# Two H3 and FFN layers on one core: block 1's odd spectra kept as doubled halves, h in two transfers, variances moved to VectorE

## The chip, the cores and the metric

The kernel runs on one core of a Trainium2 chip. The core has five engines that run in parallel, each with its own instruction queue in order: TensorE (matmuls, PE in the profile; its weight loads are shown as PEld), VectorE (DVE), ScalarE (ACT), GpSimd (POOL) and SyncE (SP), which here issues nearly all DMA transfers. Matmuls write to PSUM; VectorE or ScalarE bring the result to SBUF. The metric is the device time of one execution in microseconds; lower is better.

## The reference

A sequence of 2048 rows of 512 channels goes through two identical layers. Each is an H3 block (a gated long convolution) and a gated FFN, each behind a layer norm and added to x.

```python
    def _A_ref(q, k, v, shift_k, ssm_k, ssm_D):
        ...
        for t in range(ks):
            k_shift = k_shift + k_pad[:, t:t + S, :] * shift_k[:, ks - 1 - t][None, None, :]
        kv = k_shift * v
        ...  # y = causal convolution of kv with ssm_k along the sequence, by FFT of length 2 S
        y = y + kv * ssm_D[None, None, :]
        return q * y

    def _B_ref(x, w_gate, w_up, w_down):
        return (_silu(x @ w_gate) * (x @ w_up)) @ w_down

    x = A_q
    x = x + _A_ref(_layernorm(x, axis=-1), A_k, A_v, A_shift_k, A_ssm_k, A_ssm_D)
    x = x + _B_ref(_layernorm(x, axis=-1), B_w_gate, B_w_up, B_w_down)
    x = x + _A_ref(_layernorm(x, axis=-1), A_k, A_v, A_shift_k, A_ssm_k, A_ssm_D)
    x = x + _B_ref(_layernorm(x, axis=-1), B_w_gate, B_w_up, B_w_down)
```

The convolution y depends on k, v and the filters alone, not on x, so the kernel computes it once and uses it in both layers. S is 2048, D is 512, F is 1792, and the taps number 4.

## The kernel before, in words

**Blocks and units.** The sequence is cut into 4 blocks of 512 rows (`c` = 0 to 3; the title's block 1 is the first, index 0 in the code). A block is held as 128 partitions of 4 rows each. An FFN unit `(layer, c, h)` is two of the four rows, 256 positions: `h` = 0 the even rows 0 and 2, `h` = 1 the odd rows 1 and 3. There are 16 units; in program order block c gives (0,c,0), (0,c,1), (1,c,0), then the prologues of block c+1 in layer 0, then (1,c,1).

**The convolution.** It is done block against block with transforms as matmuls: `fwd` and `inv` are cosine and sine tables, built on the chip (L1099 to L1113, and transposed by DMA at L1158). A spectrum has four slots of a real and an imaginary part, each 128 x 512; slots 0 and 2 make one pair, 1 and 3 the other. `half` (L431) transforms two of the four rows of a block at a time: parts a and c for slots 0 and 2, b and d for slots 1 and 3, two matmuls for each part. `butterfly` (L445, L447) makes the two slots of a pair from their halves as sum and difference. `direct` (L458) makes a slot without halves, with four matmuls for each part. `product` (L642, L646, and L653 to L667 for whole spectra) multiplies the spectrum X of kv with the spectrum G of the filter into Z. `inverse_half` (L791, L797) forms in `m` the sums and differences of Z's pairs and transforms them back. The even rows need only the sums, the odd rows only the differences.

**Block 0.** Its filter h arrives by `load_h` (L342) in one transfer of 512 KB, ahead of k, v and x on SP's queue; TensorE turns it (`transpose_h`, L477) and k (`transpose_k`, L366), and multiplies the shifted k by diagonal tap matrices `dg` (`shift_mul`, L510). With `H0 = 'half'` the filter spectrum is made from halves; with `X0 = 'direct'` all four slots of X are made directly. `prologue(0, 0, 0, True)` then makes the input zT of the first unit from the even rows, turning z on TensorE (L920); other units turn z by DMA (L893). Later blocks' convolutions (`conv`) run beside the FFN of the blocks ahead of them.

**Layer norm.** `ln_stats` has VectorE gather statistics (L809, L810), add epsilon (L812), and GpSimd raise to the power -1/2 (L814, result `rstd`). `ln_stats_act`, for eight of the norms, has ScalarE do sums and squares (L828, L834) and finish the variance into `ve` (L838) ahead of GpSimd (L840).

**FFN.** For each pair of F-tiles, eight matmuls for gate and eight for up into PSUM tiles `pf` (L311); ScalarE evacuates (L970, L974), VectorE multiplies (L977), and TensorE projects down (L990). The last unit's last row goes out in two column halves, one finished by VectorE (L1008), one by ScalarE (L1011).

**Order.** Nothing is scheduled on the chip. Every operation is entered by `add`, in program order, with its engine, planned cost and buffers; `ORDER` gives each operation its rank, and each engine's queue is the operations of that engine by rank. `Plan.order` also runs through the ranks with the planned costs (`cost`, and `lat` for a transfer), which decides the buffer slot that a tile gets. `Plan.issue` fills planned TensorE gaps in the first 32 us with warm-up matmuls (`warm`, L1267) on a tile `wz`.

Of the kernel before, what the change touches and what calls it, by code (L numbers as in the profile page):

```python
# [9 lines left out]
P = 128  # L10
F32 = mybir.dt.float32
# [5 lines left out]
LN_EPS = 1e-5  # L17
# [13 lines left out]
LK0 = 4.3  # L31
HQ = 'taps'
X0 = 'direct'
# [9 lines left out]
H_SPLIT = False  # L43
# [7 lines left out]
LASTV = True  # L51
ORDER = [
# [85 lines left out]
class Plan:  # L138
# [78 lines left out]
    def issue(self, seq, place, when, warm_until, warm):  # L217
        t, busy = 0.0, {}
        for o in seq:
            start, end = when[o]  # L220
            if o.eng == "PE":
                if start < warm_until and start - t > 0.5:
                    for ring, i in [(r, i) for r in ("pf", "pd", "pc") for i in range(self.rings[r])]:
                        if busy.get((ring, i), 0.0) <= t:
                            n = int((start - max(t, 0.3) - 0.3) / 0.106)
                            if n > 0:
                                warm(ring, i, n)
                            break
# [10 lines left out]
def kernel(  # L239
# [85 lines left out]
    def fT(f, r):  # L325
        return fwd.t[:, BI[f, r], :]
# [974 lines left out]
```

## Time and profile before

| | |
|---|---|
| times of three runs | 344.28, 346.92, 723.23 us; median 346.92 |
| profiled execution | 344.93 us, of which the span from first to last instruction is 343.2 |
| granted TensorE clock | 1.00 |
| TensorE (PE) | 336.4 us busy, 98% of the span |
| VectorE (DVE) | 283.4 us busy, 83% |
| ScalarE (ACT) | 253.9 us busy, 74% |
| GpSimd (POOL) | 35.3 us busy, 10% |
| gate and up matmuls, L311 | 1792 of 256 columns |
| down matmuls, L990 | 440 seen, 102.4 us busy |

Busy time counts an instruction from its start to its end as the profile models them; neighbours on one engine overlap by a little, so the step from one to the next is shorter than one instruction's duration. In the group lines, `out<-in` are the program's tile names and `x` is a count. A wait line gives engine, line and tile that waited, then what ended it, the total in us, the number of times and the longest. A window line gives for each engine its busy time in that stretch, in the order PE, PEld, DVE, ACT, POOL, then the granted clock, the share of the DMA engines and GB/s. A timeline line gives start, duration, engine, line, operation and count; in brackets the idle time before it and what ended it.

### The profile page before, as it was taken

The numbers are of one execution on the slowest core, as the hardware profiler recorded it, in microseconds if no ns is written. First come the engines' busy times: TensorE is split into PE (matmuls) and PEld (weight loads), VectorE is DVE, ScalarE is ACT, GpSimd is POOL, SyncE is SP. The second block draws the span as 40 slices with busy tenths as digits, with TensorE's granted clock in tenths as the row PEclk, the third lists the DMA queues.
The fourth block names the chain that finished last, engine by engine and source line by source line (L and its number), as shares of the span: only waits on it lengthen the run. The fifth ranks groups of instructions, "written<-read, shape, count | busy, mean of one in ns | idle before, by whom it ended". The sixth has DMA issues, their size and how long they took to land.

```text
span 343.2 us, 6553 instructions
## 1 busy us (share of the span) xinstructions
PE 336.4 (98%) x2579; PEld 248.6 (72%) x2610; DVE 283.4 (83%) x482; ACT 253.9 (74%) x504; POOL 35.3 (10%) x46
## 2 busy tenths in 40 slices
PE   8999999999999999999999999999999999999996
PEld 7756868768687676858586777768685877777783
DVE  8899999899999999899999999989998433726022
ACT  6999999899997765958789995779475464446261
POOL 4010100203111000103110100201101001000000
PEclk9999999999999999999999999999999999999999
DMA  7999218310116044040101014210101100110101
GB/s 273 336 316 341 52 27 112 77 32 0 34 31 94 14 95 138 2 94 3 32 2 46 2 46 79 76 32 1 32 0 33 35 13 0 39 39 8 24 26 37
DMA packets 42088, 22.95 MB, mean 67 GB/s; under 512 B 33861, under 2 KB 39882, under 8 KB 42058
## 3 DMA queue, kind: packets, MB, share of 16 engines
q1 hardware_dynamic: 41904, 22.47, 26.6%
q8 instruction: 20, 0.33, 0.4%
q14 instruction: 10, 0.08, 0.1%
q10 hardware_dynamic: 154, 0.07, 0.1%
HBM read 12.33 MB, written 2.10 MB: 42 GB/s over the span
## 4 chain that ended last, share of the span: by engine, by line
PE 91%; ACT 4%; DVE 3%; issue 1%
PE pf L311 54%; PE pd L990 28%; PE ps L311 6%; PE ps L458 1%; ACT H L419 1%; PE wm L1267 1%; DVE bnst L809 1%; ACT hs L487 1%; PE pt L477 1%; ACT X L419 0%; ACT n L859 0%; PE pt L366 0%; DVE m L540 0%; DVE t L665 0%; DVE Z L667 0%
## 5 line engine op out<-in xcount | busy, mean ns | idle before, releaser
L311 PE MATMUL pf<-zT,wu_sb 128*128 128x256 bf16 x896 | 110.4, 273 | 0.1
L311 PE MATMUL pf<-zT,wg_sb 128*128 128x256 bf16 x896 | 110.2, 273 | 0.2
L990 PE MATMUL pd<-wd_sb,ht 128*128 128x512 bf16 (+1 forms) x440 | 102.4, 372 | 1.2
L311 PEld LDWEIGHTS <-wu_sb 128*128 128x128 bf16 x896 | 87.7, 98 | 16.4
L311 PEld LDWEIGHTS <-wg_sb 128*128 128x128 bf16 x896 | 87.6, 98 | 16.5 <-issue 0.8
L974 ACT CAST ht<-pf 128x512 bf16<-128x512 f32 x112 | 64.0, 591 | 29.3 <-PE pf L311 29.1
L970 ACT ACTIVATE sg<-pf 128x512 bf16<-128x512 f32 x112 | 65.5, 603 | 17.4 <-PE pf L311 15.1
L990 PEld LDWEIGHTS <-ht 128*128 128x128 bf16 x462 | 45.2, 98 | 42.5
L977 DVE TENSOR_TENSOR ht<-ht,sg 128x1024 bf16<-128x1024 bf16 (+1 forms) x64 | 39.0, 617 | 24.0 <-ACT sg L970 18.7
L814 POOL TENSOR_TENSOR rstd<-ve,nhalf 128x2 f32<-128x2 f32 x24 | 23.0, 958 | 217.8 <-DVE ve L812 207.6
L1034 ACT CAST dn<-pd 128x512 bf16<-128x512 f32 x30 | 17.0, 589 | 21.0 <-PE pd L990 20.9
L809 DVE BATCH_NORM_STATS2 bnst<-xc 128x6 f32<-128x512 bf16 x48 | 31.6, 684 | 0.6
L419 ACT ACTIVATE X<-ps 128x512 bf16<-128x512 f32 x32 | 19.2, 611 | 4.0 <-PE ps L311 3.4
L653 DVE TENSOR_TENSOR t<-X,G 128x2048 bf16<-128x2048 bf16 x18 | 21.9, 1218 | 0.1
L657 DVE TENSOR_TENSOR t<-X,G 128x2048 bf16<-128x2048 bf16 x18 | 21.9, 1216 | 0.0
L1037 DVE TENSOR_TENSOR xc<-xc,dn 128x1024 bf16<-128x1024 bf16 x15 | 10.3, 689 | 13.4 <-ACT dn L1034 13.2
L665 DVE TENSOR_TENSOR t<-t,t 128x2048 bf16<-128x2048 bf16 x12 | 14.7, 1222 | 0.3
L667 DVE TENSOR_TENSOR Z<-Z,t 128x2048 bf16<-128x2048 bf16 x12 | 14.6, 1220 | 0.2
L840 POOL TENSOR_TENSOR rstd<-ve,nhalf 128x2 f32<-128x2 f32 x8 | 8.7, 1088 | 59.2 <-ACT ve L838 59.1
L419 ACT ACTIVATE H<-ps 128x512 bf16<-128x512 f32 x24 | 13.8, 610 | 0.1
L886 DVE TENSOR_TENSOR n<-n,Yk 128x1024 bf16<-128x1024 bf16 x15 | 10.3, 688 | 4.1 <-ACT n L859 3.8
L604 ACT ACTIVATE kc<-kTb,tapF 128x512 bf16<-128x512 bf16 x16 | 12.1, 783 | 0.0
(105 smaller groups left out, 323.3 us busy)
## 6 DMA issues: line engine op xcount, KB each, us to landing
hn<-in_A_ssm_k_dram SPq DMA_DIRECT2D x4, 512.0 KB, 4.1
vt<-in_A_v_dram SPq DMA_DIRECT2D x4, 512.0 KB, 5.9
xc<-in_A_q_dram SPq DMA_DIRECT2D x4, 512.0 KB, 5.3
out_dram<-xc SPq DMA_DIRECT2D x15, 128.0 KB, 1.8
wg_sb<-in_B_w_gate_dram SPq DMA_DIRECT2D x1, 1792.0 KB
wu_sb<-in_B_w_up_dram SPq DMA_DIRECT2D x1, 1792.0 KB, 8.5
wd_sb<-in_B_w_down_dram SPq DMA_DIRECT2D x1, 1280.0 KB, 12.0
kn<-in_A_k_dram SPq DMA_DIRECT2D x1, 512.0 KB, 4.5
```

Source lines behind the costliest of these rows:

```text
L311: nc.tensor.matmul(o, lhsT=lhsT, rhs=rhs, start=(n == 0), stop=(n == len(terms) - 1))
L419: add("ACT", act(D), lambda: nc.scalar.activation(out=view(), in_=ps.t[:], func=ACT.Copy, scale=scale), r=[ps], w=[(buf, keys)], conv=conv)
L653: dve(n * D, lambda t1=t1, part=part: nc.vector.tensor_mul(out=t1.t[:], in0=x.t[:, sl, 0, :], in1=g.t[:, sl, part, :]), [(x, key(slots, (0 ...
L657: dve(n * D, lambda t2=t2, part=part: nc.vector.tensor_mul(out=t2.t[:], in0=x.t[:, sl, 1, :], in1=g.t[:, sl, 1 - part, :]), [(x, key(slots ...
L665: dve(n * D, lambda t1=t1, t2=t2, comb=comb: nc.vector.tensor_tensor(out=t1.t[:], in0=t1.t[:], in1=t2.t[:], op=comb), [t2], [t1], conv=conv)
L809: add("DVE", 0.6, lambda st=st, i=i: nc.vector.bn_stats(out=st.t[:], in_=xs[c].t[:, i, :]), r=[(xs[c], (i,))], w=[st])
L814: add("POOL", pw, lambda: nc.gpsimd.tensor_tensor(out=rstd.t[:], in0=ve.t[:], in1=nhalf.t[:].to_broadcast((P, n)), op=ALU.pow), r=[ve, nha ...
L970: add("ACT", act(D), lambda ps=ps, o=o, sg=sg: nc.scalar.activation(out=sg.t[:, o:o + 2, :], in_=ps.t[:], func=ACT.Silu), r=[ps], w=[(sg, ...
L974: add("ACT", act(D), lambda ps=ps, o=o, ht=ht: nc.scalar.copy(out=ht.t[:, o:o + 2, :], in_=ps.t[:]), r=[ps], w=[(ht, (o // 2,))], due=(uni ...
L977: dve(n * W, lambda sg=sg, ht=ht: nc.vector.tensor_mul(out=ht.t[:], in0=ht.t[:], in1=sg.t[:]), [sg], [ht], due=(unit, k / pairs, 0.0, "h"))
L990: nc.tensor.matmul((pds[o] if not cs.start else pds[HP]).t[:, cs], lhsT=ht.t[:, q, o * P:(o + 1) * P], rhs=wt["d"].t[:, ft, cs], start=(ft ...
L1034: add("ACT", act(D), lambda o=o: nc.scalar.copy(out=dn.t[:, o, :], in_=pds[o].t[:]), r=[pds[o]], w=[(dn, (o,))], due=(unit, 1.0, 3.0, "h"))
```

## The change

- `X0 = 'sum1'`: X of block 0 has slots 0 and 2 made directly as before. For slots 1 and 3 only the halves b and d are made, into `evx`, evacuated with a factor of 2. The halves of the filter, `ev`, are not combined at this point either. `pair_product` multiplies the halves themselves, b with b and d with d, into Z's slots 1 and 3. Their sum is the sum of the true products (the doubling makes up the factor), which is all that the even rows need: `inverse_sums`.
- The odd rows need the difference. `inverse_differences`, entered behind the first prologue, does the two butterflies, forms the product of slot 1 (with X still doubled, so twice the true one), takes the stored sum from it, which leaves the difference, and transforms back; then the two doubled slots of X are halved for later blocks.
- `H_SPLIT = True`: h of block 0 comes in two transfers, the second entered behind the first, and each turn of a row is two groups of transposes.
- `VE_D = True`: the variance of `ln_stats_act` is finished by VectorE.
- `TAIL = 320`: the last row's columns are cut at 320, not 256.
- The warm-up matmuls read a constant of ones in place of the tile `wz`, whose memset goes, and their number is worked out a little differently.
- Planned latencies of h, k, v and x change, and `ORDER` is a new list of 1576 ranks (1568 before).

```diff
-LK0 = 4.3
+LK0 = 3.8
-X0 = 'direct'
+X0 = 'sum1'
-H_SPLIT = False
+H_SPLIT = True
+TAIL = 320
+VE_D = True
 ORDER = [
...
-                            n = int((start - max(t, 0.3) - 0.3) / 0.106)
+                            n = int((start - t - (0.0 if 0.0 < t < 8.0 else 0.3)) / 0.106)
...
+            o = None
             for n in range(2):
...
-                        lat=LH0 - 0.75 if n == 0 else LH0 - 0.45, due=due, after=after)
+                        lat=(2.95, 3.1)[n], due=due, after=[o] if n else after)
...
+    def turn_part(m, pss, rows, slot, first):
+        for r in rows:
+            for part in (0, 1):
+                f, q = next((f, q) for f, q, t, pt in INV_TERMS[r] if t == slot and pt == part)
+                add("PE", pe(1), lambda f=f, q=q, r=r, part=part: nc.tensor.matmul(
+                    pss[r].t[:], lhsT=iT(f, q), rhs=m.t[:, slot, part],
+                    start=first and part == 0, stop=not first and part == 1),
+                    r=[(m, (2 * slot + part,)), inv], w=[pss[r]])
+
+    def inverse_sums(k):
+        y, z = new_y(k), Z[k]
+        m = spectrum("m")
+        pss = {r: new("pd", "ps", [P, D], F32) for r in (0, 2)}
+        for s in (0, 1):
+            dve(2 * D, lambda s=s: nc.vector.tensor_tensor(
+                out=m.t[:, s], in0=z.t[:, s], in1=z.t[:, s + 2], op=ALU.add), [(z, key((s, s + 2)))], [(m, key((s,)))])
+            turn_part(m, pss, (0, 2), s, s == 0)
+        fresh[k] = pss
+        evacuate_y(k, (2,))
+        return m, pss
+
+    def inverse_differences(k, m, pss):
+        z = Z[k]
+        butterfly(ev, G[0], 1, False)
+        butterfly(evx, X[0], 1, False)
+        pss.update({r: new("pf", "ps", [P, D], F32) for r in (1, 3)})
+        dve(2 * D, lambda: nc.vector.tensor_tensor(
+            out=m.t[:, 2], in0=z.t[:, 0], in1=z.t[:, 2], op=ALU.subtract), [(z, key((0, 2)))], [(m, key((2,)))])
+        turn_part(m, pss, (1, 3), 2, True)
+        pair_product(X[0], G[0], z, 1, 1)
+        dve(2 * D, lambda: nc.vector.tensor_tensor(
+            out=m.t[:, 3], in0=z.t[:, 1], in1=m.t[:, 1], op=ALU.subtract), [(z, key((1,))), (m, key((1,)))], [(m, key((3,)))])
+        turn_part(m, pss, (1, 3), 3, False)
+        evacuate_y(k, (1, 3))
+        for slot in (1, 3):
+            dve(2 * D, lambda slot=slot: nc.vector.tensor_scalar(out=X[0].t[:, slot], in0=X[0].t[:, slot], scalar1=0.5, scalar2=None, op0=ALU.mult),
+                [(X[0], key((slot,)))], [(X[0], key((slot,)))])
...
-        add("ACT", TINY, lambda: nc.scalar.activation(out=ve.t[:], in_=sm.t[:, n:2 * n], func=ACT.Identity, scale=1.0 / D, bias=eps.t[:]),
-            r=[(sm, range(n, 2 * n)), eps], w=[ve])
+        if VE_D:
+            add("DVE", 0.08, lambda: nc.vector.tensor_scalar(out=ve.t[:], in0=sm.t[:, n:2 * n], scalar1=1.0 / D, scalar2=LN_EPS,
+                                                             op0=ALU.mult, op1=ALU.add), r=[(sm, range(n, 2 * n))], w=[ve])
...
-    wz = whole("wz", [P, P])
-    add("DVE", 0.07, lambda: nc.vector.memset(wz.t[:], 0.5), w=[wz], due=-80)
+    ones = nc.const_aps.tensor(1.0, (P, P), BF16)
...
+        elif X0 == "sum1":
+            evx = spectrum("evx")
+            direct(vt[0], X[0], "pf", eng(XVE[2:4]), (2,))
+            half(vt[0], evx, "bd", 2.0, "pf", eng(XVE[4:]), False)
...
-        for slots in PAIRS:
+        for slots in PAIRS if X0 != "sum1" else ((0,), (2,)):
             product(0, 0, slots, False)
+        if X0 == "sum1":
+            for slot in (1, 3):
+                pair_product(evx, ev, Z[0], slot, slot)
...
-        if I0 == "half":
+        if X0 == "sum1":
+            m0, pss0 = inverse_sums(0)
+        elif I0 == "half":
             inverse_half(0, (0, 1))
...
     first, stats = prologue(0, 0, 0, True)
+    if X0 == "sum1" and not SUMS:
+        inverse_differences(0, m0, pss0)
...
-            for half_, (eng, cs) in enumerate((("DVE", slice(0, D // 2)), ("ACT", slice(D // 2, D)))):
+            for half_, (eng, cs) in enumerate((("DVE", slice(0, TAIL)), ("ACT", slice(TAIL, D)))):
```

More of the change, by code (lines that the diff above doesn't have):

```diff
@@ L381, in load_v @@
             return add("ACT", 0.45, lambda: nc.scalar.dma_start(out=vt[b].t[:], in_=v_t[:, b]), w=[vt[b]], lat=5.5, due=-69.5, after=[h0])
[L382 removed]
+        return add("SP", 0.6, lambda: nc.sync.dma_start(out=vt[b].t[:], in_=v_t[:, b]), w=[vt[b]], lat=(5.7, 8.6)[b] if b < 2 else 5.5, due=due, after=after)
     def load_x(c, due=None, after=()):
         xs[c] = new("x", "xc", [P, R, D], parts=R + 2)
[L386 removed]
+        return add("SP", 0.7, lambda: nc.sync.dma_start(out=xs[c].t[:], in_=q_t[:, c]), w=[xs[c]], lat=(6.2, 13.0, 5.0, 5.0)[c], due=due, after=after)
     def load_weights(which, due, after=()):
@@ L944, in ffn @@
                 i = row(h, o)
-                halves = (slice(0, D // 2), slice(D // 2, D)) if unit == LAST_UNIT and o == HP - 1 else (slice(0, D),)
+                halves = (slice(0, TAIL), slice(TAIL, D)) if unit == LAST_UNIT and o == HP - 1 else (slice(0, D),)
                 halves = [cs for cs in halves if own(o, cs)]
@@ L982, in ffn @@
                 split = unit == LAST_UNIT and o == HP - 1
-                halves = (slice(0, D // 2), slice(D // 2, D))
+                halves = (slice(0, TAIL), slice(TAIL, D))
                 cols = [[cs] for cs in halves] if last else [halves] if split else [[slice(0, D)]]
@@ L991, in go @@
                                                  start=(ft == 0 and not own(o, cs)), stop=(ft == NF - 1))
-                    add("PE", pe(n) if not last else pe(n, D // 2), go, r=[ht, (wt["d"], (0 if fts[0] == 0 else 1,))],
+                    add("PE", pe(n) if not last else pe(n, css[0].stop - css[0].start), go, r=[ht, (wt["d"], (0 if fts[0] == 0 else 1,))],
                         w=[pds[o]] if not split else [pds[o], pds[HP]] if not last else [pds[HP if css[0].start else o]],
@@ L1189 @@
             butterfly(evx, X[0], 0, False)
+        elif X0 in ("mix", "mix2"):
+            X[0] = spectrum("X0")
+            evx = spectrum("evx") if X0 == "mix" else new("t4", "evx", [P, 4, D], parts=4)
+            direct(vt[0], X[0], "pf", eng(XVE[:2]), (0,))
         else:
@@ L1194 @@
             half(hs, ev, "bd", 2.0 / N, "pf", eng(EVE[4:]), False)
-            butterfly(ev, G[0], 1, False)
+            if X0 != "sum1":
+                butterfly(ev, G[0], 1, False)
         if X0 == "half":
@@ L1266, in warm @@
         for _ in range(n):
-            nc.tensor.matmul(t[:], lhsT=wz.t[:], rhs=wz.t[:], start=True, stop=True)
+            nc.tensor.matmul(t[:], lhsT=ones, rhs=ones, start=True, stop=True)
     with tc.manual_schedule(engines={mybir.EngineType.DVE, mybir.EngineType.Activation, mybir.EngineType.PE,
```

15 lines of the change are left out of this document (10 added, 5 removed), and 116 rows, old and new, of the table ORDER.

## The prediction

> **What bounds the kernel now.** I read the page first (busy time, the 40 slices, the chain of waits), then sums by stage, then VectorE's waits, then the timeline at the first and at the last place where TensorE starts on a new block.
>
> ```profile
> PE 336.4 (98%) x2579; PEld 248.6 (72%) x2610; DVE 283.4 (83%) x482; ACT 253.9 (74%) x504; POOL 35.3 (10%) x46
> ...
> DVE  8899999899999999899999999989998433726022
> ...
> PE 91%; ACT 4%; DVE 3%; issue 1%
> ```
>
> TensorE is busy all the time and makes up 91% of the chain. But VectorE's row of tenths is 8s and 9s up to the 31st slice and falls only then. The sums by stage say it in microseconds:
>
> ```profile
> 34.00:262.00 228.00, 226.85 (x1698) 167.91 (x1718) 220.38 (x338) 186.43 (x374) 25.17 (x24) 1.00 0.21 44
> 262.00:343.20 81.20, 77.64 (x591) 58.21 (x595) 32.16 (x71) 37.91 (x69) 4.76 (x6) 1.00 0.10 27
> ```
>
> The third busy figure is VectorE: 220.38 of 228 us up to 262, then 32.16 of 81.2. So two engines are full up to 262 us, and VectorE has slack only behind that. Its queue is in order, so what is added to it early arrives at 262, unless a wait takes it up. These are its waits up to there:
>
> ```profile
> DVE ht L977 <- ACT ht L974: 1.2, 3, 0.8
> DVE kTb L374 <- PE pt L366: 1.2, 2, 0.6
> DVE z L864 <- POOL rstd L814: 0.9, 1, 0.9
> DVE n L864 <- POOL rstd L814: 0.9, 1, 0.9
> ...
> DVE n L886 <- ACT n L859: 0.6, 1, 0.6
> DVE G L447 <- ACT ev L419: 0.4, 1, 0.4
> DVE ka L608 <- ACT ka L604: 0.4, 1, 0.4
> DVE ht L977 <- ACT sg L970: 0.3, 1, 0.3
> DVE nmr L848 <- POOL rstd L814: 0.3, 1, 0.3
> ```
>
> And this is the place where 262 us counts, the first unit of block 3 in layer 0:
>
> ```profile
> 261.36 0.73 DVE L864 TENSOR_SCALAR z<-xc,mv,rstd 128x512 bf16<-128x512 bf16 x2 [0.87 <-POOL rstd L814]
> ...
> 261.84 2.50 SPq L893 DMA_TRANSPOSE zT<-z  x2
> ...
> 263.98 2.75 PE L990 MATMUL pd<-wd_sb,ht 128*128 128x512 bf16 x12
> ...
> 266.57 1.69 PE L311 MATMUL pf<-zT,wu_sb 128*128 128x256 bf16 x14
> ```
>
> VectorE writes z, SP issues the two transposes, the second at about 263.1 (half of 2.50 behind 261.84); the page gives 2.4 us to landing, so zT is there at 265.5 and TensorE takes it at 266.57. **The slack is 1.0 us.** Behind it stand four units of FFN, a unit being 112 matmuls of 0.109 us and 28 of 0.216 us, 18.2 us: 73 us that nothing shortens. Any lateness of this z over 1.0 us is a later end.
>
> **The change, part by part.** The sum is made against the profiled execution, 344.93 us: 343.2 of span and 1.7 around it. The three times shown are 344.28, 346.92 (the median) and 723.23, so the profiled one stands 0.6% under the median.
>
> TensorE, removed work. Slots 1 and 3 of the spectrum of block 0 took 2 x 2 x 4 = 16 matmuls at L458 and take 4 x 2 = 8 as halves. A step is 0.216 us (20 of them in 4.48 us): -1.73 us. The inverse keeps its 16 matmuls, but the last four of the odd rows (0.86 us) now stand behind the first FFN matmuls in ORDER.
>
> ```profile
> 4.49 1.86 PE L477 MATMUL pt<-ident,hn 128*128 128x128 bf16 x16
> ...
> 14.62 4.48 PE L458 MATMUL ps<-vt,fwd 128*128 128x512 bf16 x20
> ...
> 24.06 1.09 DVE L646 TENSOR_TENSOR Z<-t,t 128x512 bf16<-128x512 bf16 x3
> 25.18 1.89 DVE L791 TENSOR_TENSOR m<-Z 128x1024 bf16<-128x1024 bf16 x3
> ```
>
> VectorE, added work. Steps come from runs of equal instructions: three sums of 1024 end 1.89 us after the first began, one lasts 0.69, so a step is (1.89 - 0.69) / 2 = 0.60; of 512, (1.09 - 0.42) / 2 = 0.34. The product of slot 1 in `inverse_differences` is new: 2 x 0.60 + 2 x 0.34 = 1.88. The butterfly of X is new: 2 x 0.60 = 1.20. That of G is only moved behind. Two halvings of X slots, tensor_scalar of 1024 elements: not in the trace in this shape. Two z of 512 elements take 0.73, so their step is 0.33, and a sum of 1024 takes 0.60; I take 0.46, the middle, as both rows are equally near: 0.92, bounds 0.66 and 1.20. Eight variances now done here: L812, the same form, lasts 0.17 and steps at about 0.08: 0.64, at most 1.36. The memset of wz goes: -0.17. Sum **+4.5 us, bounds 4.2 to 5.5.** The Trainium skill, "VectorE: DVE Perf Modes", section "The perf-mode tier table", lists a tensor_scalar on bf16 in SBUF at about twice the rate of a tensor_tensor (693 against 1224 ns for 2048). By it a halving is an estimated 0.35 us and the sum 4.25; the 1218 ns of L653 here agree for the two-source side.
>
> From the lists of ORDER, read against the operations in program order, VectorE's queue ahead of z of unit (0,3,0) also gains one addition of L1037 (0.6 net). So z meets **5.0 us more VectorE work (4.7 to 6.0)**.
>
> What pays it back. (1) At the head: h in halves lets the first transposes start on 256 KB. The first of the 16 began at 4.49 and they took 1.86, so starting half of them earlier is worth up to 0.9. It costs one more SP issue of 0.45 us, behind which k, v, x, h1, v1, wg and the inverse tables are queued; the DMA engines are full there (share 1.0 from 2.5 us on), so their landing is set by bytes. VectorE's three waits there are 0.6 + 0.6 + 0.4 = 1.6. Against it stands a new wait: the first variance waits in VectorE's queue for ScalarE's second Square and its read, with the products of pair 3 behind it, and these need the new halves that ScalarE evacuates right after. I price it at 0.5 (0 to 1.6) and credit the head with 1.2 (0 to 1.6, and 0 if both h halves land together). (2) Waits on ScalarE from 34 to 262, 1.2 + 0.6 + 0.4 + 0.3 = 2.5 and some of under 0.3 each: a queue that comes later finds these done. I take 2.2 (0 to 2.8). (3) Waits on POOL's rstd, 0.9 + 0.9 + 0.3 = 2.1: these are answers to VectorE's own variance and vanish only where ORDER puts other work in between. It does so at the two long ones (an ht product and the L1037 addition ahead of this z). I take 1.4 (0 to 2.1). Together 4.8 (0 to 6.5), so z is later by 5.0 - 4.8 = **+0.2 us (-1.8 to +6.0)**, and with 1.0 of slack the unit may start 0.8 earlier.
>
> TensorE's own count agrees. In the head VectorE's queue up to z of unit (0,0,0) is 0.6 us shorter (the difference sums and half a butterfly go behind it), and with 1.2 less waiting z comes 1.8 earlier than 31.45; I take the first FFN matmul 1.5 earlier than 33.58. The 0.86 us moved behind it come off again: -0.6. Both ways the end moves by 0.6 to 0.8.
>
> The small parts. The tail: ScalarE's last copy shrinks from 256 to 192 columns (0.37 us now, 0.61 for 512 in rows like it): -0.06, and VectorE's larger piece becomes the peer: -0.05. ScalarE loses 8 x 0.29 = 2.3 us of variances; it is 73% busy or more, and what hides that is TensorE's own queue, so nothing. Warm-up matmuls on a constant start with the barrier instead of behind the memset, 0.2 earlier: nothing, since they end when data comes. Changed lat figures act only through ORDER and slots.
>
> Sum: 344.93 - 0.8 - 0.05 = 344.1; I say **344.0 us**.
>
> **The rivals.**
> Repaid in full (342.0): every wait vanishes and the head gains 3 us. TensorE then saves its 1.73 and 1.2 of head. For it: TensorE waited for VectorE almost nowhere before. Against: the 1.0 us of slack, and VectorE's queue would have to take up 6 us of waits.
>
> Not repaid (349.0): one mechanism at one place, the z of unit (0,3,0). If VectorE still waits as now, z is 5.0 late, TensorE stands 4.0 and the end is 344.93 + 4.0; 349.9 with the upper prices. It is slower from a net lateness of 1.0 us on. For it: two engines full up to 262, and four VectorE chains per block whose gaps of 0.03 us remain. Against: waits on others shrink when one's own queue is late.
>
> The clock (343.1). Warm-up and transposes before 7 us step at about 0.10 us (16 in 1.86, one lasting 0.3), 64 later ones at 0.06 (3.74 us). If earlier warm-up opened the fast step before the h transposes, 24 transposes save 24 x 0.045 = 1.1 us and VectorE's two waits at L374 go: 0.9 under my sum. The Trainium skill, "TensorE: Matmul & The Clock Gate", section "What's actually happening", says the gate opens after a busy window of about 3.4 us that runs free of the program; here the slow step lasted from 1.04 to about 7.2, nearly two such windows, so a start 0.2 earlier may or may not win one.
>
> The split does nothing (345.2): both halves land with the last byte, since k is queued on the same full DMA engines. The head's 1.2 falls away: 344.1 + 1.2 - 0.1.
>
> **How the numbers follow.** My forecast 0.48 (its own range 343.0 to 346.5), repaid in full 0.17, the clock 0.10, no effect of the split 0.05, not repaid 0.20. The range 341.5 to 349.5 leaves out the lower end of the second case and the upper half of the last. About 2% (6.9 us) is what a measurement of this kernel can tell from no change. Faster by more needs under 338: 0.05, out of the full repayment. Slower by more needs 352, z late by 8 us: over my upper price for one unit, but the same squeeze may cost at several; 0.10, out of "not repaid". The same: 0.85.
>
> **What would show it.** In the changed profile: 16 matmuls at the direct line instead of 32, and 8 of halves; VectorE's busy sum at about 288; its waits up to 262 at half of now; first FFN matmul at 32.1; z of unit (0,3,0) at about 261.6 and TensorE's start on it near 265.8; no TensorE gap over 0.5 us before it. A gap of several microseconds there, or at the start of another unit, proves me wrong on the slow side. An end under 342 would mean that VectorE was not the second bound.

## The result, and the profile after

Over 22 runs each the changed kernel took 346.90 us in the median (344.71 to 348.96) and the kernel before 344.44 us (343.59 to 346.92, and one run of 723.23); the ratio is **1.0066, 95% interval 1.0051 to 1.0081**: slower by 2.3 us where 0.9 faster was forecast. The profiled execution took 347.71 us, 345.8 of them span, against 344.93 and 343.2. The median lies inside the outer range of the prediction, 341.5 to 349.5, but no case of which that range was made names what made it late.

The page of the changed kernel, to set beside that of before (engine, busy us, share of the span, instructions; the tenths of the granted clock in 40 slices; the shares of the chain):

```profile
PE 336.7 (97%) x2583; PEld 248.4 (72%) x2615; DVE 285.4 (83%) x497; ACT 251.2 (73%) x496; POOL 38.7 (11%) x46
...
PEclk9899999999999999999999999999999999999999
...
PE 74%; ACT 11%; DVE 10%; DMA 2%; issue 1%; POOL 1%; SPq 0%
```

VectorE has 285.4 us, 2.0 more than before; the forecast said 288. The chain has changed more than the sums: TensorE's share falls from 91% to 74%, a transfer is in it with 2%, and the second slice of the clock row is no longer 9. The sums by stage (PE, PEld, DVE, ACT, POOL, then clock, DMA share, GB/s) say where:

```profile
0.00:34.00 34.00, 29.93 (x285) 21.40 (x290) 28.08 (x71) 26.87 (x56) 5.34 (x15) 0.95 0.98 315
34.00:262.00 228.00, 226.39 (x1696) 167.47 (x1716) 221.97 (x349) 184.26 (x371) 27.90 (x23) 1.00 0.20 44
262.00:345.80 83.80, 80.33 (x608) 59.58 (x612) 35.39 (x79) 40.06 (x72) 5.49 (x8) 1.00 0.11 26
```

Up to 34 us TensorE is busy for 29.93 us (31.95 before) and the clock stands at 0.95. From 34 to 262 the line is that of before: TensorE 226.39 (226.85), VectorE 221.97 (220.38). So in this execution the loss is at the head. TensorE's first 12 us, on the timeline (start, duration, engine, line, operation, count; in brackets the idle time before it and what ended it):

```profile
3.74 1.91 PE L481 MATMUL pt<-ident,hn 128*128 128x128 bf16 x16
5.45 0.66 PE L1335 MATMUL wm<-const-bfloat16-1.0 128*128 128x128 bf16 x6
8.15 1.07 PE L370 MATMUL pt<-ident,kn 128*128 128x128 bf16 x16 [2.04 <-DMA kn<-in_A_k_dram]
...
9.78 2.77 PE L313 MATMUL ps<-hs,fwd 128*128 128x512 bf16 x6 [0.22 <-issue]
```

h's transposes began at 3.74 in place of 4.49, as intended. Then come 6 warm-up matmuls, **2.04 us of nothing until k lands**, 16 fast transposes of k, and six matmuls of 512 columns in 2.77 us, 0.45 us each in place of 0.22. The window lines of these stretches give the clock beside it:

```profile
8.00:10.00 2.00, 1.63 (x18) 1.31 (x20) 1.29 (x2) 1.19 (x3) 0.00 (x0) 0.79 1.03 396
10.00:13.00 3.00, 3.00 (x12) 1.29 (x11) 1.38 (x2) 1.08 (x3) 0.00 (x0) 0.57 1.04 415
13.00:16.00 3.00, 2.95 (x47) 2.68 (x47) 2.40 (x4) 2.76 (x8) 0.00 (x0) 1.00 1.22 391
```

0.79, then 0.57 for three microseconds, then 1.00. The first FFN matmul starts at 35.38 (before: 33.58; forecast: 32.1), and z of unit (0,3,0), at 261.36 before:

```profile
264.17 0.41 DVE L913 TENSOR_SCALAR z<-xc,mv,rstd 128x512 bf16<-128x512 bf16 x1
```

It is 2.8 late, TensorE starts on it at 269.28 in place of 266.57, and the end is 2.6 later. Of that, 1.80 was there at the first FFN matmul, and 2.67 at the second unit (55.81 against 53.14): the difference is that of the inverse matmuls (0.86 us) that were moved behind the first.

### The profile page after: what moved, and what is told of

It reads as the page before. It is cut to its first block, busy times and chain, and to the rows that moved or that the text cites. A ratio compares the mean times of both kernels' runs of the same rounds, so it can differ in the third digit from the quotient of the medians.

```text
span 345.8 us, 6581 instructions
## 1 busy us (share of the span) xinstructions
PE 336.7 (97%) x2583; PEld 248.4 (72%) x2615; DVE 285.4 (83%) x497; ACT 251.2 (73%) x496; POOL 38.7 (11%) x46
## 4 chain that ended last, share of the span: by engine, by line
PE 74%; ACT 11%; DVE 10%; DMA 2%; issue 1%; POOL 1%; SPq 0%
PE pf L313 43%; PE pd L1039 24%; PE ps L313 5%; DMA kn<-in_A_k_dram 2%; DVE bnst L854 2%; ACT ht L1023 2%; ACT sg L1019 1%; ACT n L908 1%; DVE m L544 1%; PE ps L462 1%; DVE t L657 1%; ACT H L423 1%; DVE t L661 1%; ACT X L423 1%; DVE t L669 1%
## 5 line engine op out<-in xcount | busy, mean ns | idle before, releaser
L313 PE MATMUL pf<-zT,wg_sb 128*128 128x256 bf16 x896 | 111.1, 273 | 0.1
L313 PE MATMUL pf<-zT,wu_sb 128*128 128x256 bf16 x896 | 109.2, 273 | 0.5 <-DVE zT L972 0.4
L1039 PE MATMUL pd<-wd_sb,ht 128*128 128x512 bf16 (+2 forms) x440 | 101.8, 372 | 1.1
L313 PEld LDWEIGHTS <-wg_sb 128*128 128x128 bf16 x896 | 87.6, 98 | 17.4 <-issue 0.4
L313 PEld LDWEIGHTS <-wu_sb 128*128 128x128 bf16 x896 | 87.5, 98 | 16.1 <-issue 1.1
L1019 ACT ACTIVATE sg<-pf 128x512 bf16<-128x512 f32 x112 | 66.6, 607 | 31.7 <-PE pf L313 29.9
L1023 ACT CAST ht<-pf 128x512 bf16<-128x512 f32 x112 | 65.3, 591 | 15.4 <-PE pf L313 12.6
L859 POOL TENSOR_TENSOR rstd<-ve,nhalf 128x2 f32<-128x2 f32 x24 | 24.3, 1015 | 213.1 <-DVE ve L857 171.6
L423 ACT ACTIVATE X<-ps 128x512 bf16<-128x512 f32 x28 | 17.2, 626 | 5.7 <-PE ps L313 4.9
L889 POOL TENSOR_TENSOR rstd<-ve,nhalf 128x2 f32<-128x2 f32 x8 | 10.8, 1347 | 62.5 <-DVE ve L884 62.5
L313 PE MATMUL ps<-hs,fwd 128*128 128x512 bf16 x36 | 13.0, 425 | 1.0 <-ACT hs L491 0.7
```

What stands on the lines that cost most here:

```text
L313: nc.tensor.matmul(o, lhsT=lhsT, rhs=rhs, start=(n == 0), stop=(n == len(terms) - 1))
L423: add("ACT", act(D), lambda: nc.scalar.activation(out=view(), in_=ps.t[:], func=ACT.Copy, scale=scale), r=[ps], w=[(buf, keys)], conv=conv)
L859: add("POOL", pw, lambda: nc.gpsimd.tensor_tensor(out=rstd.t[:], in0=ve.t[:], in1=nhalf.t[:].to_broadcast((P, n)), op=ALU.pow), r=[ve, nha ...
L1019: add("ACT", act(D), lambda ps=ps, o=o, sg=sg: nc.scalar.activation(out=sg.t[:, o:o + 2, :], in_=ps.t[:], func=ACT.Silu), r=[ps], w=[(sg, ...
L1023: add("ACT", act(D), lambda ps=ps, o=o, ht=ht: nc.scalar.copy(out=ht.t[:, o:o + 2, :], in_=ps.t[:]), r=[ps], w=[(ht, (o // 2,))], due=(uni ...
L1039: nc.tensor.matmul((pds[o] if not cs.start else pds[HP]).t[:, cs], lhsT=ht.t[:, q, o * P:(o + 1) * P], rhs=wt["d"].t[:, ft, cs], start=(ft ...
```

## The experiments

Theory 1: the second transfer of h makes k late, TensorE waits and then runs slowly. Theory 2: VectorE's added work costs it, unit by unit. Theory 3, added behind the first four runs: GpSimd's rstd is held up behind VectorE. Each kernel stood in one job with the kernel before; the ratio is to that. "k" is k's place among SyncE's transfers and its time from issue to landing in the profiled execution; "clock" counts the runs with a granted share of 0.995 or less over the whole run; "rstd" is the length of that of unit (1,0,0), near 60 us. Single runs of one kernel differ by up to 4.4 us, so the medians decide, and a profiled execution shows one of them. In e6, e10 and e12 the second of SyncE's transfers is a row of 1 KB. The lines of these kernels lie up to 3 beside those of the changed kernel (L311 is its L313).

| run | median us (runs) | ratio, 95% | k: place, us | first FFN | rstd | clock |
|---|---|---|---|---|---|---|
| before, profiled | | | 2nd, 4.5 | 33.58 | 1.79 | |
| after | 346.90 (22) | 1.0066, 1.0051 to 1.0081 | 3rd, 6.4 | 35.38 | 2.20 | 10 |
| e1 one h | 345.87 (12) | 1.0020, 1.000 to 1.004 | 2nd, 4.5 | 31.89 | 2.20 | 0 |
| e2 ev first | 346.65 (12) | 1.0032, 1.0008 to 1.0056 | 3rd, 5.2 | 32.31 | 2.20 | 0 |
| e3 before, split | 346.56 (12) | 1.0052, 1.0029 to 1.0075 | 3rd, 5.7 | 34.37 | 1.80 | 3 |
| e4 more warm-up | 347.21 (12) | 1.0062, 1.0035 to 1.0088 | 3rd, 6.1 | 33.42 | 3.93 | 0 |
| e5 spectra only | 347.76 (6) | 1.0081, 1.0063 to 1.0099 | 2nd, 4.6 | 31.63 | 2.13 | 5 |
| e6 late k | 344.88 (12) | 1.0013, 0.9988 to 1.0039 | 3rd, 4.0 | 31.35 | 2.20 | 3 |
| e7 h on ScalarE | 346.55 (12) | 1.0049, 1.0031 to 1.0067 | 2nd, 4.5 | 33.94 | 2.20 | 2 |
| e8 before, variances | 349.13 (6) | 1.0134, 1.011 to 1.0159 | 2nd, 4.9 | 35.13 | 1.06 | 0 |
| e9 e4 and copy | 346.26 (9) | 1.0051, 1.0034 to 1.0067 | 3rd, 5.7 | 33.07 | 0.69 | 0 |
| e10 e6, ev first | 345.27 (12) | 1.0023, 1.0003 to 1.0043 | 3rd, 6.5 | 32.76 | 3.93 | 0 |
| e11 k between | 346.68 (6) | 1.0066, 1.0043 to 1.009 | 2nd, 4.7 | 34.35 | 3.93 | 0 |
| e12 e10 and copy | 344.67 (11) | 1.0008, 0.9994 to 1.0022 | 3rd, 5.8 | 32.26 | 0.69 | 0 |
| **e13 e1 and copy** | 344.35 (12) | 0.9989, 0.9975 to 1.0003 | 2nd, 4.6 | 31.47 | 0.69 | 0 |
| e14 e13, ev first | 345.03 (12) | 1.0007, 0.9993 to 1.002 | 2nd, 4.8 | 32.31 | 0.69 | 0 |
| e15 after and copy | 347.57 (6) | 1.0074, 1.0046 to 1.0102 | 3rd, 5.8 | 35.57 | 0.69 | 3 |
| e16 e5 and two copies | 344.49 (12) | 1.0005, 0.9993 to 1.0016 | 2nd, 4.6 | 31.64 | 0.69 | 0 |
| **e17 e13 again** | 344.16 (12) | 0.9978, 0.9961 to 0.9994 | 2nd, 4.4 | 32.00 | 0.69 | 0 |
| e18 before and copy | 344.63 (12) | 0.9993, 0.9977 to 1.0009 | 2nd, 4.9 | 33.09 | 0.69 | 0 |

**The first four: which part.** In e1 and e3 one constant is turned and the ranks of h's load and transposes in ORDER follow it.

```diff
e1 (changed kernel)      e3 (kernel before)
-H_SPLIT = True          -H_SPLIT = False
+H_SPLIT = False         +H_SPLIT = True
```

> The changed kernel with one part undone: block 0's h comes in one transfer again (one issue on SyncE ahead of k's, four whole transposes in place of eight halves); all other parts stay. Theory 1 (the head: the second transfer delays k, TensorE waits 2.0 us for it and then runs slowly): k is issued at 1.24 us instead of 1.73 and lands by 6.5 instead of 8.15, the wait of 2.0 us on kn is below 0.7, the first FFN matmul starts at 33.6 or before (35.4 in the changed kernel), and the time is 344.3 to 345.0, at least 1.8 below the changed kernel. Theory 2 (VectorE's added work, met at every unit): the first FFN matmul comes no more than 0.5 earlier and the time is 346.4 to 347.2.

> The kernel before with one part of the change: h in two transfers, the second ahead of k, the four transposes as eight halves; spectra, variances, warm-up operand and tail as before. Theory 1: the loss is in this part alone: k lands 0.5 to 2 us later than in the kernel before, TensorE waits for it, the first FFN matmul starts 1 to 2 us later than 33.58 and the time is 345.4 to 346.4. Theory 2: no VectorE work is added, so the time is 344.0 to 344.8.

The split alone costs the kernel before 0.52%, 1.8 us, as theory 1 had it (346.56 is 0.2 over its range); taking it out of the changed kernel brings the ratio from 1.0066 to 1.0020, 1.6 us. The head of e1 is better than expected and about what the prediction had said:

```profile
6.35 1.06 PE L368 MATMUL pt<-ident,kn 128*128 128x128 bf16 x16
7.25 1.89 PE L311 MATMUL ps<-hs,fwd 128*128 128x512 bf16 x7
```

k's transposes follow h's with no gap, the matmuls of 512 columns behind them run at the full step, and the first FFN matmul comes at 31.89. But e1's median is 345.87, above the 345.0 expected at most: something else costs 1 us.

e2 changes ranks of ORDER alone: the four `half` operations of h's even pair (L435) and their evacuations stand ahead of `transpose_k`.

> The changed kernel, h still in two transfers and k still issued behind both, but in TensorE's order the eight half matmuls of h's even pair (L435, ev) and their evacuations stand ahead of the sixteen transposes of k. Theory 1: k still lands near 8.1, but some 1.8 us of matmuls now lie in the wait: the wait of 2.0 us on kn falls below 0.8, the first FFN matmul starts near 33.9, the time is about 345.3. Theory 2: the first FFN matmul within 0.5 of 35.4 or the gain is given back by unit (0,3,0); the time stays at 346.4 to 347.2.

The wait on k is gone though k took 5.2 us, no run lost the clock, and the first FFN matmul came at 32.31. The ratio fell by a third of a per cent only (1.0066 to 1.0032; the median is 346.65 where 345.3 was expected), while the profiled execution, at 344.62, is one of the best two; what its other runs lack its trace cannot show. e4 keeps TensorE busy without work:

```diff
-LK0 = 3.8
+LK0 = 6.4
```

> The changed kernel with 31 warm-up matmuls instead of 6 between the transposes of h and those of k (k's planned latency 6.4 instead of 3.8), so that TensorE does not stand still while k is under way. Nothing of the work is earlier. If the clock that drops after the idle 2.0 us is a part of the loss, the 512-column matmuls of 9.8 to 12.6 us have a step of 0.22 instead of 0.43, the first FFN matmul comes 1.0 to 1.5 earlier (34.0 to 34.4) and the time is 345.4 to 345.9. If the wait alone is the loss, the first FFN matmul stays at 35.2 to 35.6 and the time at 346.5 to 347.2.

The clock held in all 12 runs and the first FFN matmul came 2.0 earlier, more than expected. Yet the median is 347.21, and the runs fall into two groups, 345.6 to 346.6 and 347.8 to 349.6. In the profiled one, of the upper group, TensorE stood still for 1.27 us at 66.56. The chain there goes back over ScalarE to GpSimd. GpSimd's instruction, then VectorE's at the same time:

```profile
60.19 3.93 POOL L889 TENSOR_TENSOR rstd<-ve,nhalf 128x2 f32<-128x2 f32 x1 [13.86 <-DVE ve L884]
```

```profile
59.95 0.16 DVE L884 TENSOR_SCALAR ve<-sm 128x2 f32<-128x2 f32 x1
60.02 0.68 DVE L561 TENSOR_TENSOR X<-m 128x1024 bf16<-128x1024 bf16 x1
60.62 1.22 DVE L666 TENSOR_TENSOR Z<-t,t 128x2048 bf16<-128x2048 bf16 x1
61.75 0.68 DVE L1026 TENSOR_TENSOR ht<-ht,sg 128x1024 bf16<-128x1024 bf16 x1
62.35 1.22 DVE L661 TENSOR_TENSOR t<-X,G 128x2048 bf16<-128x2048 bf16 x1
```

A reciprocal root of two columns takes 0.69 us where nothing is beside it. Here it took 3.93, and ended 0.6 behind the fourth of VectorE's two-input operations, when VectorE itself had run out of work. In e1 the same instruction took 2.20 and slipped in behind the second of them. The Trainium skill, "SBUF — State Buffer", section "Who interferes with whom", says that a VectorE instruction with two SBUF inputs contends with a GpSimd instruction that reads SBUF, and calls the pair of ports that the two engines share an exclusive lock. The trace agrees: in e4, in e1 and in the kernel before, this rstd ends 0.55 us behind the end of a two-input operation, whichever it got in behind. That several such instructions in a row can keep GpSimd out, and that this changes from run to run, is what these runs add.

**The next four: single parts and the order of transfers.**

```diff
e5, on e1
-VE_D = True
+VE_D = False
e8, on the kernel before
-        add("ACT", TINY, lambda: nc.scalar.activation(out=ve.t[:], in_=sm.t[:, n:2 * n], func=ACT.Identity, ...
+        add("DVE", 0.08, lambda: nc.vector.tensor_scalar(out=ve.t[:], in0=sm.t[:, n:2 * n], scalar1=1.0 / D, ...
```

> The changed kernel with two parts undone: h in one transfer, as in e1, and the eight variances of ScalarE's statistics finished on ScalarE again, each right behind its sums (eps is then needed, as before). What is left of the change are the spectra, the warm-up operand and the tail. Theory 3 (the variance on VectorE is followed at once by VectorE's own two-input operations, and GpSimd's rstd, which reads it, stands still while these run: 3.93 us for the one at 60.2 us in e4, 2.20 in e1, 1.79 in the kernel before): the rstd of 58 to 62 us takes at most 1.8, and the time is 0.5 to 1.0 below e1's 345.87, thus 344.8 to 345.4. Theory 2 (VectorE's added spectra work is what is left of the loss): removing 0.6 us of small VectorE operations changes little, 345.6 to 346.0. If the variances were a gain, as the prediction had it (1.4 us of rstd waits repaid), the time rises to 346.3 or more.

> The kernel before with one part of the change alone: the eight variances of ScalarE's statistics on VectorE, at the same ranks of the order. Theory 3: the eight rstd of line 840 take longer (median 1.00 us and longest 1.79 in the kernel before; 1.31 and 2.20 to 3.93 in kernels with the variances on VectorE), and the time is 0.3 to 1.2 above the kernel before of the same job. The prediction's reading: rstd comes earlier, and the time is 0 to 1.4 below. Theory 2: no difference, since the spectra are not touched.

Neither is a clean answer on the variances, and theory 3 missed both. In e5 the rstd near 60 us still took 2.13 (1.8 at most was expected) and the time lies over every range given but that of the variances as a gain; rstd of unit (0,0,1) took 4.04 us, TensorE stood still for 2.16 at 42.04 and the clock fell to 0.81 from 44 to 50. In e8 the ranks are those of ScalarE's operations, and VectorE waits there for the sums:

```profile
DVE ve L838 <- ACT jk L834: 4.9, 3, 1.8
```

So e8's 4.2 us say more of the place than of the variance; its own rstd near 60 took 1.06 only. In its profiled execution, at 351.0 the slowest of six, the rstd at 112.1 us took 10.53, behind a row of twelve two-input operations of VectorE's.

e6 and e7 ask what delays k.

```diff
e6, on e1
-        dr = add("ACT", 0.42, lambda: nc.scalar.dma_start(out=drow.t[0:1, :], ...
+        dr = add("SP", 0.42, lambda: nc.sync.dma_start(out=drow.t[0:1, :], ...
e7, on the changed kernel
-                o = add(eng, 0.5, lambda sl=sl: q.dma_start(...
+                o = add(("SP", "ACT")[n], 0.5, lambda sl=sl, n=n: (nc.sync, nc.scalar)[n].dma_start(...
```

> e1 (h in one transfer) with one move: the 1 KB transfer of D's row is issued by SyncE between h and k in place of by ScalarE, so that k is issued some 0.5 us later, as in the changed kernel, while h stays whole. If the late issue alone makes k slow, k takes 5.2 to 6.4 us from its issue, as in the four kernels with two transfers, TensorE waits for it and the time is 346.5 to 347.2. If it is the two transfers of h themselves, k takes 4.5 us as in e1, lands 0.5 later than there, TensorE waits at most 0.3 and the time is 345.8 to 346.3.

> The changed kernel with the second half of h issued by ScalarE (behind tapR, ahead of D's row) in place of SyncE, so that k is issued by SyncE at 1.24 us again; h is still two transfers. If the late issue is what delays k, k lands by 6.5, TensorE does not wait for it, and the time is that of e1 or up to 0.5 below, 345.4 to 345.9. If the two transfers themselves slow the DMA engines, k takes over 5.2 us from its issue, lands at 6.5 to 7.5, TensorE waits 0.4 to 1.4 and the time is 346.3 to 347.

e6 by itself spoke for the halves as the cause (k 4.0 us although issued at 1.67), and its median is 0.9 below what was expected for that. But e10 and e12 have the same first transfers as e6, h whole and k third, and k took 6.5 and 5.8 there. In e7 k was in time, 4.5 us; now the half on ScalarE's queue came late, and TensorE waited 0.47 and 1.13 us for h; the time lies in the range for slow halves, but k was not slow. So neither reading held alone, and e11 puts k between the halves: one rank of SyncE's, and the `after` of the second half and of k.

> The changed kernel with SyncE's order h first half, k, h second half. In the four kernels where k was SyncE's third transfer the rate fell to 36 to 121 KB in the half microsecond from 4.0 us, where k's packets begin, against 185 to 206 with h whole. If it is the third large transfer that starts badly, k now takes at most 4.5 us from 1.24 and the second half of h is late (over 4.5 us from its issue at 1.74), TensorE waits for h instead, over 1 us, and the time is 346.3 to 347.3. If the halves themselves are slow, k takes over 5 us again and the time is 347 or more. If neither, both land by 6.2 and the time is 345.0 to 345.9.

k took 4.7 (4.5 expected), the second half, third now, was late, and TensorE waited 1.36 for it; the time is in the range given for "it is the third". Over all profiles: **k as SyncE's second transfer took 4.4 to 4.9 us in eleven of eleven; as its third 5.2 to 6.5 in eight of nine,** and 4.0 in e6. The rate in 40 slices of 0.3 us from 0 to 12 shows the hole, first the changed kernel (with the busy tenths of the DMA engines), then e1:

```profile
DMA  0000002699999923966689999899999999999999
GB/s 0 0 0 0 0 10 72 225 358 359 358 318 174 123 82 150 259 218 205 259 328 382 355 382 369 328 423 393 399 382 396 372 389 420 413 427 403 408 456 401
```

```profile
GB/s 0 0 0 0 0 14 55 133 304 352 341 335 478 410 423 437 341 68 137 246 300 369 423 423 369 396 369 372 386 375 382 430 434 403 399 422 422 415 454 418
```

The 13th to 15th value, from 3.6 us: 174, 123, 82 against 478, 410, 423. In the first two of these slices the engines are busy 9 tenths of the time all the same. There the packets of k, 4096 bytes, begin in the changed kernel; single ones take up to 1213 ns in place of 159. e1 has such a hole too, at the 18th value (68), where v begins, SyncE's third there; nothing waits for v. Why the third transfer starts so is open. A late issue alone is 0.5 us; but in all nine the third place goes together with an issue at 1.67 to 1.74 us in place of 1.24, and no run separates the two.

**GpSimd set free.** One instruction is added: a copy that makes VectorE wait for that rstd.

```diff
+        if key_ == (1, 0, 0):
+            fence = whole("fence", [P, n], F32)
+            add("DVE", 0.1, lambda: nc.vector.tensor_copy(out=fence.t[:], in_=rstd.t[:]), r=[rstd], w=[fence])
         return nm, rstd
```

> e4 (the changed kernel with 31 warm-up matmuls ahead of k) with one added instruction: behind the variance of unit (1,0,0) VectorE makes a 2-column copy of rstd, and so does nothing of its own until GpSimd has finished that rstd. Theory 3 in its general form (GpSimd's rstd stands still while VectorE runs two-input operations back to back; whether it slips in between two of them changes from run to run): the rstd that took 3.93 us from 60.2 takes at most 1.1, the runs of 347.8 to 349.6 of e4 (6 of 12) vanish, and the median falls from 347.2 to 345.7 to 346.4. If the long rstd is not what makes those runs slow, both groups of times stay, 1 us later for the pause of VectorE, and the median is 347 to 348.2.

```profile
59.80 0.69 POOL L887 TENSOR_TENSOR rstd<-ve,nhalf 128x2 f32<-128x2 f32 x1 [13.85 <-DVE ve L882]
...
60.52 0.17 DVE L891 COPY fence<-rstd 128x2 f32<-128x2 f32 x1 [0.80 <-POOL rstd L887]
```

rstd takes 0.69, VectorE pauses for 0.80, and all of e9's runs lie between 346.0 and 346.8: e4's upper group is gone. e10 and e12 repeat it on another base.

> e6 (the changed kernel with h in one transfer and D's row issued by SyncE) with the order of e2: the half matmuls of h's even pair and their evacuations ahead of the transposes of k. Theory 1 with the clock: e6 showed a granted share of 0.995 in 3 of 12 runs, all of them over 347 us, so TensorE still stands still on k in some runs; with work in that place none is left at 0.995, the runs over 346.5 go, and the median falls from 344.9 to 344.0 to 344.6. If these runs have another cause, 2 or 3 of 12 stay over 347 and the median is within 0.4 of 344.9.

> e10 with the one added copy of e9. If the long rstd of unit (1,0,0) comes up in e10 as well, its slow runs go and the median is 0.2 to 0.6 below e10's. If it does not, VectorE's pause of about 1 us costs 0 to 0.8 and the median is at or above e10's.

In e10 five of 12 runs stand at 346.2 to 346.8; the profiled one (346.67) has an rstd of 3.93. In e12 it is 0.69, and the runs span 344.5 to 345.3. So e10's expectation missed: no run was at 0.995, the clock held, and the upper runs were rstd's. The other profiles fit: the third with 3.93, e11's at 348.73, is the only one of its six runs above 346.9, while with 2.20 the profiled executions of e1, e2 and e6 are the fastest or next to it of their kernels.

**Both causes out.** e13 is e1 with the copy, e14 has the order of e2 as well, e15 is the changed kernel with the copy, e16 is e5 with two (`key_ in ((1, 0, 0), (0, 0, 1))`).

> e1 (the changed kernel with h in one transfer, k SyncE's second transfer) with the one added copy of e9 behind the variance of unit (1,0,0). Theory 3: the slow group of e1 (its runs of 346.3 to 347.3) goes; with k early (4.5 us from 1.24) the median is 344.2 to 344.8, at most as in e12, against 345.9 for e1. If k's arrival is all there is, the copy costs up to 1 us and the median is 345.9 to 346.9.

> e13 with the order of e2 (the half matmuls of h's even pair ahead of the transposes of k). With k here by 5.8 us there is no wait left to cover: within 0.3 of e13, with fewer runs above the median if k is late in some runs; 344.2 to 344.8.

> The changed kernel itself with the one added copy behind the variance of unit (1,0,0). Theories 1 and 3 together: the long rstd is gone, but k is still SyncE's third transfer, TensorE still waits for it and the granted share still falls to 0.995 or less in about half of the runs; the median is 345.9 to 346.5, between e9's 346.3 and the changed kernel's 346.9. If theory 3 carries most of the changed kernel's loss, the median is 345.5 or less; if none, 346.9 to 347.9.

> e5 (h in one transfer, the eight variances on ScalarE) with the added copy behind the variances of units (0,0,1) and (1,0,0). e5 lost 2 us against e1, and in its trace the rstd at 35.6 us took 4.04. If that rstd is its whole loss, the variances themselves are worth nothing, and the median is within 0.5 of e13. If the variances on VectorE are a gain of their own, as the prediction had it, the median is 1.0 or more above e13.

e13 is as expected, 344.35. e14 is 0.7 above it, where at most 0.3 was expected: with k in time, the order of e2 only makes k's transposes later (8.0 in place of 5.9). e16 is within 0.5 of e13, so e5's loss was its rstd, with the clock that fell behind it, and **the variances on VectorE are worth 0.1 us by the medians, 0.6 by the ratios**, with one pause of VectorE more in e16. e15 missed: 347.57 with the copy. Three of its six runs lost the clock. In the profiled one the row of the clock shows 9s throughout, but the steps tell more; e15, then e9, which differs by 25 warm-up matmuls:

```profile
5.03 1.26 PE L479 MATMUL pt<-ident,hn 128*128 128x128 bf16 x10 [0.22 <-DMA hn<-in_A_ssm_k_dram]
6.08 0.84 PE L1336 MATMUL wm<-const-bfloat16-1.0 128*128 128x128 bf16 x6
7.62 1.89 PE L368 MATMUL pt<-ident,kn 128*128 128x128 bf16 x16 [0.70 <-DMA kn<-in_A_k_dram]
...
10.16 2.66 PE L311 MATMUL ps<-hs,fwd 128*128 128x512 bf16 x6 [0.22 <-issue]
12.65 0.39 PE L311 MATMUL ps<-dg,kTb 128*128 128x128 bf16 x4
```

```profile
4.52 0.75 PE L479 MATMUL pt<-ident,hn 128*128 128x128 bf16 x10 [0.28 <-DMA hn<-in_A_ssm_k_dram]
5.11 1.99 PE L1336 MATMUL wm<-const-bfloat16-1.0 128*128 128x128 bf16 x31
...
8.43 1.89 PE L311 MATMUL ps<-hs,fwd 128*128 128x512 bf16 x8
```

In e15 ten transposes of h take 1.26, 16 of k 1.89, six matmuls of 512 columns 2.66: the slow step lasts until 12.65. In e9 ten transposes of h take 0.75, 31 warm-up matmuls 1.99 and eight matmuls of 512 columns 1.89: the fast step is there from 4.5 on. That is 2.5 us at the first FFN matmul and 0.8 us by the ratios (1.0074 against 1.0051). So in the changed kernel the wait and the slow step come first, and taking out the long rstd alone gains nothing that six runs show.

> e13 once more, to narrow its interval: if its advantage over the kernel before is real, the median is again 0.1 to 0.6 below that of the kernel before in the same job; if it was chance, within 0.1 or above.

> A control: the kernel before with the added copy of rstd of unit (1,0,0) in VectorE's queue, behind the first product that runs beside that rstd. In the kernel before this rstd took 1.79 us in the profiled execution, and 6 of 35, 1 of 29 and 2 of 29 of its runs stood at 346.5 or more. If the copy helps any kernel of this kind, it also takes these runs away and the median is 0 to 0.4 lower; if the long rstd concerns the changed order alone, the pause of VectorE costs 0 to 1 us and the median is 344.5 to 345.5.

e13 again is faster than the kernel before, 0.9978 with an interval below 1; the two jobs give 0.25 and 0.7 us. The copy alone brings the kernel before nothing that the interval shows.

## Why the prediction was wrong, point by point

**The step that failed is point (1) of the repayment: the second issue of h costs nothing because "the DMA engines are full there, so their landing is set by bytes".** In the profiled execution k landed 2.4 us later (8.1 against 5.7) behind the same bytes. From 3 to 6 us, before the change and after, the last two figures are the share of the DMA engines and GB/s:

```profile
3.00:6.00 3.00, 2.94 (x30) 2.58 (x28) 2.79 (x12) 2.00 (x5) 1.81 (x3) 1.00 1.02 352
```

```profile
3.00:6.00 3.00, 3.00 (x32) 2.63 (x29) 2.85 (x15) 2.66 (x8) 1.80 (x3) 1.00 0.80 215
```

So the engines were neither full nor, where they were busy, moving bytes at their rate: a share of busy time does not say that bytes alone set a landing. The trace of before held the warning: its rate also dips, to 259 GB/s at 5.4 us, where v was SyncE's third transfer. The prediction credited the head with 1.2 and bounded it at 0 from below; the split alone measured 1.8 us of loss. Nor did it read the new ORDER for what stands in TensorE's queue behind a late k: all 16 transposes stood ahead of the matmuls on h, where the kernel before had eight, with matmuls on h in between.

**The clock** was a rival only as a gain. It went the other way: in 10 of 22 runs the granted share fell to 0.995 or less, and these have a median of 347.9 against 346.1 for the other 12. With 31 warm-up matmuls in the wait (e4) or matmuls on h (e2) none of 12 fell. The Trainium skill, "TensorE: Matmul & The Clock Gate", section "What's actually happening", says that the gate closes after an idle window of about 3.4 us and that the window runs free of the program. The second agrees with a wait that closes the gate in some runs only; on the first the measurement decides: here 2.04 us were enough, and 2.16 in e5. The counts leave out runs in which the fast step only came late, since their share can stand at 1.00 (e15).

**For the rest of the head the number was right, its ground was not.** With k in time (e1, e6, e13, e17) the first FFN matmul starts at 31.35 to 32.00; 32.1 was forecast. But these kernels have h in one transfer, and the prediction had put 1.2 us of its gain down to the two; without them it gave 345.2. The 1.73 us of matmuls taken out, which the forecast did not add, are of the size of what came instead; no run takes them out alone. Of the 2.1 us won in e13, 1.25 are left at unit (0,0,1) and 1.3 at (0,3,0): the 0.86 us of matmuls moved behind come off, as the sum had it.

**VectorE.** The halvings last 0.42 and 0.40 us, with 0.33 and 0.31 from the start of each to that of the next instruction. At 0.46 a step they were priced too high, and the estimate of 0.35 by the Trainium skill, "VectorE: DVE Perf Modes", section "The perf-mode tier table", was nearer. z of unit (0,3,0) was to come at 261.6: in e1 it starts at 261.02 (before: 261.36), and in e13 at 260.16. So "not repaid" did not happen and theory 2 is out. But the terms were wrong by more than their difference. VectorE's busy time, the third busy figure, up to this z in the kernel before and in e1:

```profile
0.00:261.36 261.36, 258.16 (x1986) 190.04 (x2012) 250.60 (x410) 215.55 (x435) 30.54 (x40) 1.00 0.32 80
```

```profile
0.00:261.02 261.02, 257.20 (x1993) 189.98 (x2020) 252.23 (x425) 211.88 (x426) 34.24 (x39) 1.00 0.31 80
```

It rose by 1.6 us where 5.0 was forecast, and VectorE's idle time ahead of z fell by 2.0 where 4.8 was. That the two errors cancel is luck. The durations of its instructions up to there, added one by one, do rise by about 5 us (275.0 to 280.2): in the new order more of them overlap with the next, which the prediction, pricing the added instructions alone, did not count. Of the waits credited, those on GpSimd's rstd fell from 2.1 to 0.6, as forecast; those on ScalarE, credited with 2.2, rose from 3.3 to 4.1 in e1's list:

```profile
DVE ht L1024 <- ACT sg L1017: 0.9, 3, 0.4
...
DVE n L933 <- ACT n L906: 0.8, 1, 0.8
DVE xc L1084 <- ACT dn L1081: 0.7, 1, 0.7
DVE n L911 <- POOL rstd L887: 0.6, 1, 0.6
```

All waits listed did not halve: 7.4 before, 6.1 in e1, 5.9 in e13 with the copy's 0.8. In the changed kernel they are 9.7, because of the head:

```profile
DVE kTb L378 <- PE pt L370: 1.8, 1, 1.8
DVE ev L426 <- PE ps L313: 1.2, 2, 1.0
...
DVE G L449 <- ACT ev L423: 0.8, 1, 0.8
```

**POOL's rstd.** The prediction saw VectorE's waits for it, not that its duration depends on VectorE, though the rows of before have 0.69 to 1.79 for one shape, and not that ScalarE, and TensorE behind it, wait for it too (e4). It costs 1.1 us between e1 and e13.

**The sum.** h in two transfers, and with them the third place of k: 1.0066 to 1.0020, +1.6 us. Long rstd: 1.0020 to 0.9989, +1.1. What is left, 0.9989 and 0.9978: -0.4 and -0.8, where the prediction had -0.9 for the whole; this is h in one transfer and with the copy, and **it is the version that beats both kernels**, by 0.1 to 0.2%; the interval of e13 still touches no change (1.0003), that of e17 does not (0.9994). The shares hold in this order of taking out only: with k late the copy gained nothing (e15).

## What to carry to other kernels

Before a load is cut in two, count what the second issue does to the place of every transfer behind it, and look at what is queued behind the one that becomes late; an order tuned to planned landings has no slack for 2 us. Small GpSimd operations on a critical chain are priced with the VectorE operations that run beside them, and where these have two SBUF inputs a pause of 0.8 us in VectorE can be cheaper than the lottery. Judge such a change by a set of runs: one profiled execution of e2 (344.62) would have told the opposite of its median (346.65).

## What the runs showed of the hardware that was not expected

- SyncE's third transfer: 5.2 to 6.5 us for 512 KB in eight of nine profiles, 4.4 to 4.9 as the second in eleven of eleven.
- One GpSimd instruction on 128x2 took 0.69 to 10.53 us, by what VectorE ran beside it; those of 1.79 us and more that stand here ended 0.55 us behind the end of a two-input operation of VectorE.
- TensorE's fast step first came at 4.5 us (e9) or at 12.65 (e15) with the same warm-up up to 5 us, while the row of the granted clock showed 1.00 in both: the row shows a clock that falls back (0.57 in the changed kernel), not one that has not risen yet.
